# The start of a two-branch kernel: first input tile in halves on two queues, its transposes in four PSUM banks, identity built on chip, initial memory transposed behind the first tile, one norm put off

## Chip, cores and metric

One core of one Trainium2 chip. The metric is the device time of the whole program in microseconds (us); lower is better. Time before the change: median 1509.06 us of three runs when the prediction was made. All runs told here were classed as fast. The mean granted TensorE clock (the share of its full speed that the profile shows PE was allowed) was 1.0 in most; it was 0.994 to 0.999 in all runs of r3, r5 and r8, in three of five of r7, and in single runs of r4, r6 and of before. The profiled runs among these show what that mean hides: before the last microseconds, one stretch at half clock, of 3.4 us (10.2 us in r5), that begins during a wait of PE or within 1.2 us after one (waits of 0.9 to 9.5 us). Work that falls into 3.4 us at half clock is done 1.7 us later. Where this bears on a comparison it is said.

## The reference, cut to what matters

```python
def reference(A_x, A_mem0, A_Wq, ..., B_w1, B_w2, B_w3, B_w4):
    x = A_x                                   # (1, 2048, 1024) bf16
    xn = _layernorm(x)
    return x + _A_ref(xn, A_mem0, ...) + _B_ref(xn, B_w1, ...)

def _B_ref(x, w1, w2, w3, w4):                # gets xn, and norms it once more
    h  = _gelu(_layernorm(x) @ w1)            # 1024 -> 1024
    hs = shift_tokens(h) @ w2                 # four groups of columns, by -1, +1, -2, +2 tokens
    x1 = x + hs
    return x1 + _gelu(_layernorm(x1) @ w3) @ w4          # 1024 -> 3584 -> 1024

def _A_ref(x, mem0, Wq, Wk, Wv, Wo, seg_len): # attention by segments of 32 tokens,
    ...                                       # 8 memory rows handed from segment to segment, mem0 first
```

The kernel calls the first branch B and runs it first. I call its parts **stage one** (norm, transpose, times w1, GELU; 0 to 67 us), **stage two** (times w2, second norm; 67 to 122 us) and **stage three** (times w3 and w4, from 122 us on, with the first work of branch A in between). Branch A fills the rest up to 1504 us and is not touched, but for where its initial memory comes from. A tile is 128 tokens; there are 16.

## The kernel before

A tile of x goes through statistics on VectorE (DVE), one power -1/2 on GpSimd (POOL), and two norms: `norm2` (layer norm of the layer norm, the input of w1) and `norm1` (xn itself, kept in SBUF and also stored to a scratch in DRAM, for branch A). For tiles 0 to 5 TensorE (PE) transposes norm2's result against an identity; from tile 6 on a DMA does it, issued by SyncE (SP).

```python
    ident = const_tile("c_ident", np.eye(P, dtype=np.float32))     # loaded from DRAM
    load_consts(1)
    ...
    sums = cpool.tile([P, NTILE * 8, 4], F32)
    nc.gpsimd.memset(sums[:], 1.0)
    ...
    load_x(0)                                                      # SP's queue, one 128x1024 tile
    for c, q in ((0, nc.scalar), (2, nc.scalar), (1, nc.sync), (3, nc.sync)):
        if q is nc.sync:
            load_x(1 + c // 2)
        q.dma_start(w1_sb[:, 2*c:2*c+2, :], w1_v[:, 2*c:2*c+2, :])  # w1 in four quarters
    ...
    def norm_stats(n, part=None):
        ...
        nc.vector.scalar_tensor_tensor(ab[:], epsm[:], mv[:, 1:2], epsa[:], op0=ALU.mult, op1=ALU.add)
        nc.gpsimd.tensor_tensor(rr[:], ab[:], neghalf[:], op=ALU.pow)   # both columns at once

    def norm2(n, xn2T, jj):
        ...                                          # DVE for tiles 0-7, ScalarE (ACT) from tile 8 on
        if n >= NPE:                                 # NPE = 6
            nc.sync.dma_start_transpose(xn2T[:, jj], xn2[:])

    def norm1(n):
        ...
        nc.vector.tensor_scalar(xn, xts[n][:], mv[:, 0:1], rr[:, 0:1], op0=ALU.subtract, op1=ALU.mult)
        nc.gpsimd.dma_start(xn_v[:, n, :], xn)       # the store, 256 KB
        ...

    def transposes(xn2, xn2T, jj, half, halves=False):
        ps = psum0.tile([P, 4, P], F32, tag="tr")    # one bank for four transposes, two such banks
        for k in range(4):
            nc.tensor.matmul(ps[:, k, :], xn2[:, ...], ident[:], start=True, stop=True)
        step = 2 if halves else 4
        for i in range(0, 4, step):
            nc.scalar.copy(xn2T[:, jj, half*4+i:half*4+i+step, :], ps[:, i:i + step])
    ...
    def ahead(n):                                    # n = 6, 7
        norm_stats(n + 1, 0)
        norm2_of(n)
        norm_stats(n + 1, 1)
        norm1(n - 2)
    def prep(n):                                     # n = 8 .. 15
        norm2_of(n)
        norm_stats(n + 1)
        norm1(n - 2)
    ...
    def mem_start():                                 # in stage three, at about 219 us
        ps9 = psum3.tile([P, KT, M + 1], F32, tag="vr")
        for k in range(KT):
            nc.tensor.matmul(ps9[:, k, :], m0[:, k*P:(k+1)*P], eye9[:], start=True, stop=True)
        ...
```

## Time and profile before

| | before |
|---|---|
| time, median of 3 | 1509.06 us (1509.02 to 1513.19) |
| time, median of all 6 runs beside the changed kernel's | 1509.69 us |
| span of the profiled run | 1507.1 us |
| PE busy | 1497.1 us, 99% |
| waits of PE | three, all before 33 us |
| first weight matmul | 7.99 us |
| second tile's first weight matmul | 12.01 us |
| third wait of PE | 0.54 us, ends at 32.20 |
| stage two starts | 67.13 us |
| stage three starts | 122.39 us |

PE is the bound nearly everywhere, so a microsecond of this kernel is won only if PE starts its matmuls earlier, waits less between them, or has fewer of them. The lines of the profile are in the prediction and are not shown again. In a timeline line the columns are: start and busy time in us, engine, line of the kernel, operation, output<-input, shapes, count, and in brackets the idle time before it and what ended that. In a line of waits they are: engine, tile and line that waited, what it waited for, then us in total, number of waits and the longest.

### The profile page before, as it was taken

The page shows a single profiled execution, that of the slowest core. Times are in us where ns is not written, and L with a number is a line of the kernel's source. Part 1 is how long each engine was busy: PE and PEld are TensorE (multiplying, and loading weights), DVE is VectorE, ACT ScalarE, POOL GpSimd, SP SyncE. Part 2 cuts the span into 40 slices and gives each one's busy share as a digit, 9 for nine tenths or more (in the row PEclk, how much of TensorE's full clock was granted, in tenths as well). Part 3 has the DMA queues.
Part 4 walks back from the last instruction along what each step waited for, and adds up shares of the span by engine and source line. Part 5 has one row for each costly group of instructions (what it writes and reads, how often), then busy time and mean ns, then how long its engine had stood idle before and what let it go on. Part 6 is the DMA issues. An engine that isn't in the chain of part 4 may idle for free.

```text
span 1507.1 us, 24242 instructions
## 1 busy us (share of the span) xinstructions
PE 1497.1 (99%) x9757; PEld 803.3 (53%) x9828; DVE 546.9 (36%) x1146; ACT 502.0 (33%) x1140; POOL 176.6 (12%) x247
## 2 busy tenths in 40 slices
PE   9999999999999999999999999999999999999999
PEld 7844444445454444444456645664665455545555
DVE  8382230100010112211246624651564166516642
ACT  5533103013012011111156614650663166406630
POOL 5241020211211221100000000001000100010001
PEclk9999999999999999999999999999999999999999
DMA  9699752453445777622389956992997298918911
GB/s 307 156 272 321 218 174 89 137 203 111 155 155 144 188 236 252 218 98 84 126 219 262 238 128 174 255 239 72 240 251 203 72 230 217 223 63 207 209 49 51
DMA packets 305410, 272.93 MB, mean 181 GB/s; under 512 B 156054, under 2 KB 272312, under 8 KB 305296
## 3 DMA queue, kind: packets, MB, share of 16 engines
q1 hardware_dynamic: 282800, 189.38, 50.4%
q0 software_dynamic: 21808, 80.85, 15.4%
q8 instruction: 79, 1.29, 0.4%
q10 hardware_dynamic: 688, 1.11, 0.2%
q14 instruction: 35, 0.29, 0.1%
HBM read 190.08 MB, written 45.29 MB: 156 GB/s over the span
## 4 chain that ended last, share of the span: by engine, by line
PE 98%; DVE 1%; issue 0%; DMA 0%; ACT 0%; POOL 0%
PE ps L658 30%; PE ps L592 15%; PE pso L716 15%; PE ps L533 13%; PE ps L559 13%; PE ps L397 4%; PE ps L315 3%; PE psS L673 2%; PE psO L697 2%; PE ps L856 1%; PE ps L485 1%; PE gps L468 0%; PE ps L454 0%; DVE st L256 0%; DVE st L259 0%
## 5 line engine op out<-in xcount | busy, mean ns | idle before, releaser
L658 PE MATMUL ps<-hTb,wt 128*128 128x396 bf16 (+2 forms) x2528 | 484.9, 342 | 0.0
L658 PEld LDWEIGHTS <-wt 128*128 128x128 bf16 x2528 | 236.7, 98 | 175.7 <-DMA wt<-in_A_Wq_dram 0.4
L592 PE MATMUL ps<-wt,xT 128*128 128x512 bf16 x1004 | 220.1, 379 | 1.1
L716 PE MATMUL pso<-wo_sb,oX 128*128 128x512 bf16 (+1 forms) x972 | 208.3, 372 | 1.1
L533 PE MATMUL ps<-xn3T,w_sb 128*128 128x512 bf16 x896 | 196.2, 379 | 0.0
L559 PE MATMUL ps<-w_sb,h3T 128*128 128x512 bf16 x873 | 194.1, 379 | 1.2
L592 PEld LDWEIGHTS <-xT 128*128 128x128 bf16 x1024 | 100.2, 98 | 120.8
L534 ACT ACTIVATE h3T<-ps 128x512 bf16<-128x512 f32 x112 | 66.9, 597 | 291.1 <-PE ps L533 290.2
L716 PEld LDWEIGHTS <-oX 128*128 128x128 bf16 x992 | 96.3, 98 | 107.6
L660 ACT CAST KT<-ps 128x462 bf16<-128x462 f32 (+2 forms) x160 | 81.8, 511 | 202.8 <-PE ps L658 198.7
L559 PEld LDWEIGHTS <-h3T 128*128 128x128 bf16 x896 | 87.1, 98 | 103.6
L533 PEld LDWEIGHTS <-w_sb 128*128 128x128 bf16 x896 | 86.6, 98 | 102.0
L679 DVE TENSOR_REDUCE sums<-sm 99x4 f32<-99x396 f32 (+2 forms) x176 | 97.6, 555 | 114.9 <-ACT sm L677 114.9
L662 ACT ACTIVATE QT<-ps 128x462 bf16<-128x462 f32 (+2 forms) x160 | 83.9, 525 | 120.3 <-PE ps L658 106.2
L594 ACT CAST Vs<-ps 128x512 bf16<-128x512 f32 x64 | 37.5, 586 | 232.1 <-PE ps L592 223.5
L675 DVE TENSOR_TENSOR sm<-psS,c_mask_reg_sb 99x396 f32<-99x396 f32 x152 | 86.7, 571 | 72.0 <-PE psS L673 71.7
L598 DVE CAST Vs<-ps 128x512 bf16<-128x512 f32 x64 | 44.3, 692 | 171.6 <-PE ps L592 166.0
L677 ACT ACTIVATE sm<-sm 99x396 f32<-99x396 f32 (+2 forms) x176 | 92.8, 527 | 34.9 <-DVE sm L675 27.9
L685 DVE TENSOR_TENSOR Pn<-sm,rs 99x396 bf16<-99x396 f32 (+2 forms) x176 | 98.9, 562 | 6.4 <-DVE rs L681 0.5
L723 POOL DMA_DIRECT2D out_dram<-ot x30 | 16.4, 548 | 698.2 <-DVE ot L722 698.1
L560 DVE TENSOR_TENSOR R<-ps,R 128x512 f32<-128x512 f32 x32 | 22.0, 690 | 182.1 <-PE ps L559 172.5
L722 DVE TENSOR_TENSOR ot<-pso,Rt 128x512 bf16<-128x512 f32 (+1 forms) x33 | 22.2, 675 | 166.6 <-PE pso L716 162.3
(127 smaller groups left out, 1049.5 us busy)
## 6 DMA issues: line engine op xcount, KB each, us to landing
wt<-in_A_Wq_dram SPq DMA_DIRECT2D x76, 512.0 KB
wt<-in_A_Wk_dram SPq DMA_DIRECT2D x76, 512.0 KB
wt<-in_A_Wv_dram POOLq DMA_DIRECT2D x24, 1024.0 KB, 6.4
V_scratch<-Vs SPq DMA_DIRECT2D x32, 512.0 KB
V<-V_scratch SPq DMA_DIRECT2D x40, 384.0 KB
R_scratch<-x POOLq DMA_DIRECT2D x16, 512.0 KB, 4.1
R<-R_scratch SPq DMA_DIRECT2D x16, 512.0 KB
R_scratch<-R POOLq DMA_DIRECT2D x16, 512.0 KB, 3.5
```

Source lines behind the costliest of these rows:

```text
L533: nc.tensor.matmul(ps[:].rearrange("p (n t) -> p n t", t=P), w3_sb[:, k, f * P:(f + 1) * P], xn3T[tb][:, :, k, :], start=(k == 0), stop=(k ...
L534: nc.scalar.activation(h3T[:, f, :], ps[:], ACTF.Gelu_apprx_tanh)
L559: nc.tensor.matmul(ps[:], h3T[:, f, j * P:(j + 1) * P], w4_sb[:, f, ch * 512:(ch + 1) * 512], start=(f == 0), stop=(f == FT - 1))
L592: nc.tensor.matmul(ps[:], xT[:, m4 * 4 + j, k, :], wv[:, k, :], start=(k == 0), stop=(k == KT - 1))
L658: nc.tensor.matmul(ps[:, :nb], w[:, k, hh * P:(hh + 1) * P], B["hT"][:, k, :nb], start=(k == 0), stop=(k == KT - 1))
L660: nc.scalar.copy(dst[:, hh, :], ps[:, :nb])
L662: nc.scalar.mul(dst[:, hh, :], ps[:, :nb], scale)
L675: nc.vector.tensor_tensor(sm[:T, :, :T], S3, t["mask"][:].unsqueeze(1).to_broadcast((T, 4, T)), op=ALU.add)
L677: nc.scalar.activation(e[:T, :, :T], sm[:T, :, :T], ACTF.Exp, scale=LN2)
L679: nc.vector.tensor_reduce(ss, e[:T, :, :T], axis=AX.X, op=ALU.add)
L685: nc.vector.tensor_tensor(Pn[:T, :, :T], e[:T, :, :T], rs[:T, :].unsqueeze(2).to_broadcast((T, 4, T)), op=ALU.mult)
L716: nc.tensor.matmul(self.ps[:, :self.w], self.oX[0][:, h, self.oX[1] + self.gl * P:self.oX[1] + (self.gl + 1) * P], wo_sb[:, h, self.cc], s ...
```

## The change

The intent is to get PE to its first real matmul sooner, and to take eight small matmuls out of stage three. The diff, without the declarations:

```diff
-    ident = const_tile("c_ident", np.eye(P, dtype=np.float32))
-    load_consts(1)
-    eye9 = const_tile("c_eye9", ...)
+    ident = cpool.tile([P, P], BF16)
+    nc.vector.memset(ident[:], 1.0)
+    eye9 = cpool.tile([M, M + 1], BF16)
+    c0 = cpool.tile([P, KT, 1], F32)
...
-    nc.gpsimd.memset(sums[:], 1.0)
...
-                psum0 = ... tc.tile_pool(name="psum0", bufs=2, space=PSUM)
+                psum0 = ... tc.tile_pool(name="psum0", bufs=4, space=PSUM)
...
-                            nc.sync.dma_start(xts[n][:], x_v[:, n, :])
+                            if n == 0:
+                                nc.scalar.dma_start(xts[n][:, 512:], x_v[:, n, 512:])
+                                nc.sync.dma_start(xts[n][:, :512], x_v[:, n, :512])
+                            else:
+                                (nc.gpsimd if n == 12 else nc.sync).dma_start(xts[n][:], x_v[:, n, :])
+                    m0 = hTB[:M, 0, 16:16 + D]
+                    nc.gpsimd.dma_start(m0, A_mem0[0])
+                    nc.gpsimd.affine_select(ident[:], ident[:], [[-1, P]], ALU.is_equal, 0.0, base=0, channel_multiplier=1)
+                    nc.gpsimd.memset(eye9[:, M:M + 1], 1.0)
+                    nc.gpsimd.tensor_copy(eye9[:, 0:M], ident[:M, :M])
...
-                        nc.gpsimd.tensor_tensor(rr[:], ab[:], neghalf[:], op=ALU.pow)
+                        for c in (slice(1, 2), slice(0, 1)) if n == 0 else (slice(0, 2),):
+                            nc.gpsimd.tensor_tensor(rr[:, c], ab[:, c], neghalf[:, c], op=ALU.pow)
...                                                   # transposes():
-                        ps = psum0.tile([P, 4, P], F32, tag="tr")
-                        for k in range(4):
-                            nc.tensor.matmul(ps[:, k, :], ...)
                         step = 2 if halves else 4
                         for i in range(0, 4, step):
-                            nc.scalar.copy(..., ps[:, i:i + step])
+                            ps = psum0.tile([P, 4, P], F32, tag="tr")
+                            for k in range(step):
+                                nc.tensor.matmul(ps[:, k, :], ...)
+                            nc.scalar.copy(..., ps[:, :step])
...                                                   # behind tile 0's transposes:
+                    for k in range(KT):
+                        nc.tensor.matmul(ps9[:, k, :], m0[:, k * P:(k + 1) * P], eye9[:], start=True, stop=True)
                     norm_stats(1)
+                    nc.vector.tensor_copy(MZ[:, :, 0:M], ps9[:, :, 0:M])
+                    nc.vector.tensor_copy(c0[:], ps9[:, :, M:M + 1])
-                    load_consts(5)
+                    load_consts(4)
+                    nc.gpsimd.memset(sums[:], 1.0)
...                                                   # ahead(n):
-                        norm1(n - 2)
+                        if n == 6:
+                            norm1(n - 2)
...                                                   # prep(n):
+                        if n == 8:
+                            norm1(n - 3)
                         norm1(n - 2)
...                                                   # stage three:
+                    if n == 0:
+                        nc.vector.tensor_tensor(xb[:, :, 0:1], c0[:], xb[:, :, 0:1], op=ALU.add)
-                m0 = ...                              # and its load
-                def mem_start(): ...                  # and its call
```

`norm1(5)` is the norm put off: it now stands directly before `norm1(6)`.

> **What bounds the kernel now.** First the page of the profile: busy shares and the shares of the chain.
>
> ```profile
> PE 1497.1 (99%) x9757; PEld 803.3 (53%) x9828; DVE 546.9 (36%) x1146; ACT 502.0 (33%) x1140; POOL 176.6 (12%) x247
> PE 98%; DVE 1%; issue 0%; DMA 0%; ACT 0%; POOL 0%
> ```
>
> PE is busy for 1497.1 us of a span of 1507.1 us, so all that any rearrangement can win is about 10 us, or 0.7%. The change leaves the matrix work of the stages alone. Next I asked which waits of PE there are at all in the whole span:
>
> ```profile
> PE warm L332 <- DVE wz L326: 1.4, 1, 1.4
> PE ps L292 <- DVE xn L271: 0.8, 1, 0.8
> PE ps L315 <- ACT hTB L317: 0.5, 1, 0.5
> ```
>
> Three, and all lie in the first 33 us. The other idle time is a few ns between matmuls and the last 3 us (the output's way out), which the change does not touch. So the question is how early PE gets its real work, and what becomes of the third wait. The timeline of the head:
>
> ```profile
> 4.03 0.69 DVE L256 BATCH_NORM_STATS2 st<-xt 128x6 f32<-128x512 bf16 x1 [2.71 <-DMA xt<-in_A_x_dram]
> 5.91 0.73 POOL L262 TENSOR_TENSOR rr<-ab,neghalf 128x2 f32<-128x2 f32 x1 [3.30 <-DVE ab L261]
> 6.67 0.73 DVE L271 TENSOR_SCALAR xn<-xt,mv,rr 128x512 bf16<-128x512 bf16 x2 [0.85 <-POOL rr L262]
> 7.14 0.72 PE L292 MATMUL ps<-c_ident_sb,xn 128*128 128x128 bf16 x8 [0.79 <-DVE xn L271]
> 7.57 1.20 ACT L295 CAST xn2T<-ps 128x256 bf16<-128x256 f32 x4 [4.31 <-PE ps L292]
> 7.99 2.84 PE L305 MATMUL ps<-xn2T,w_sb 128*128 128x128 bf16 x48
> ...
> 12.20 0.53 POOL L130 DMA_DIRECT2D c_mask_sb<-c_mask  x1
> 12.74 0.74 POOL L262 TENSOR_TENSOR rr<-ab,neghalf 128x2 f32<-128x2 f32 x1
> ...
> 13.51 0.55 DVE L271 TENSOR_SCALAR xn<-xt,mv,rr 128x1024 bf16<-128x1024 bf16 x1 [0.75 <-POOL rr L262]
> ...
> 24.96 3.97 SPq L275 DMA_TRANSPOSE xn2T<-xn  x2
> ...
> 30.64 1.24 ACT L273 ACTIVATE xn<-xt,nm,rr 128x1024 bf16<-128x1024 bf16 x1 [2.05 <-DVE mv L260]
> ...
> 32.20 35.09 PE L315 MATMUL ps<-xn2T,w_sb 128*128 128x256 bf16 x320 [0.54 <-ACT hTB L317]
> ```
>
> The serial head is: x tile 0 lands at 4.01, two statistics, one power on POOL, the norm, transposes, a copy, and the first weight matmul at 7.99. After 13.51 DVE has no gap until 31 us. It feeds tiles 6 and 7, whose DMA transposes start at 24.96 and 27.64. By the semaphores in the trace these land at 30.54 and 31.88. ACT's norm of tile 8 starts 0.1 us after the first landing. The profile names DVE's aggregate as its releaser, but that ended at 30.61, after ACT's wait had already been answered by the landing. That norm (1.24 us) holds up the copies out of PSUM behind it on ACT, and PE resumes at 32.20, just after a copy that ended at 32.15. So the third wait hangs on DVE's chain through the DMA transposes. From 32.20 on PE runs without a gap: an earlier head is worth only as much as 32.20 moves.
>
> **What the Trainium skill says.** "DMA: Bandwidth & Descriptors", section "Issuing engines are not separate DMA queues": queues of several engines run on the same 16 DMA engines, and issuing from two saves only the sequencer's time. The trace agrees in part. The issues of x tile 0 (SP) and the first weights (ACT) both start at 0.76, yet between 2 and 3 us the transfers by queue are
>
> ```profile
> q1 hardware_dynamic: 85, 0.17, 75.0%
> q10 hardware_dynamic: 2, 0.00, 2.9%
> ```
>
> (q1 is SP's). ACT's queue moves only when SP's tile is nearly through.
>
> "GPSIMD Engine Reference", section "2.1 Instruction dispatch": each POOL instruction pays two software dispatches, and the first call to freshly loaded code about 6 us. The first half agrees: a power of two columns takes 0.70 to 0.98 us here, one of one column 0.56 to 0.57 (the third norm at 72 us and later). The second is not seen: POOL changes its configuration at 2.53, and the power still starts 0.08 us after its input at 5.82.
>
> "PSUM — Partial Sum Buffer", section "Terms": TensorE and ScalarE must not touch one bank at once. The trace agrees as far as it goes: the first copy starts at 7.57, after the fourth transpose of its bank ended at 7.53.
>
> "TensorE: Matmul & The Clock Gate", Part 1: full rate comes after some 3.4 us of activity. The 12 warming matmuls start every 0.43 us (slow), and the transposes at 7.14 take 219 ns (fast).
>
> **The change part by part.**
>
> *x tile 0 in halves.* It removes no bytes. The 128 rows took from 1.75 to 3.3 us on the wire, only some 85 a microsecond, against about 200 a microsecond later. Half rows might make the first half land some 0.3 us earlier, but there are twice as many rows, and the second half comes from the queue that started last. First statistic up to 0.3 us earlier; the second may wait for its half. I take 0.2 us won (estimate; -0.3 to +0.5 is open).
>
> *Power by column, the needed one first.* About 0.73 - 0.57 = 0.16 us won. The other column runs on POOL before tile 1's statistics are there (7.3 to 9.1 us), so it costs nothing.
>
> *Identity built on chip.* The loaded one landed at 6.62, 0.5 us before its use. It would have become a floor under any larger gain; by itself it wins nothing. The fill of 128x128 goes ahead of the warming fill on DVE (256 words took 0.27 us), so the warm-up ends some 0.1 us later, at about 6.6: still before the transposes at about 6.8.
>
> *Four banks.* The first copy can start after two transposes instead of four: 2 x 56 ns = 0.11 us earlier, 7.99 becomes 7.88.
>
> *Initial memory behind the first tile.* Eight tiny matmuls. Their cost in the old place, from the chain:
>
> ```profile
> 219.24 0.28 PE ps L442 x8
> ```
>
> With the issue step of 0.05 us about 0.33 us leave PE's gapless stretch: a true win. In the new place they stand on PE between the last transpose (its next slot is 7.69) and the first weight matmul: 7.69 + 0.28 = 7.97. They eat what the four banks won (7.97 against 7.99). DVE's two copies (0.21 and about 0.18 us) fit in its 0.82 us wait for tile 1's power.
>
> *POOL's order.* One small constant load (0.63 us) goes, the fill of the sums (0.71 us, formerly in the dead time at 1.90) comes in before tile 2's power, which already waits for POOL: 13.51 would come some 0.15 us later relative to the rest (2.27 + 0.71 against 2.81, with the first load of a row dearer). That is lost from DVE's chain.
>
> *Norm put off.* Tile 5's second norm (0.54 us) stands after tile 7's norm on DVE, so it does not move the two transposes. The chain shown by the profile runs through it, but I read ACT's wait as the landing. I give it 0.
>
> *x tile 12 by POOL's queue*: 0.6 us of POOL in a slack place; 0.
>
> Sum: DVE's chain 0.20 + 0.16 - 0.15 = 0.21 us earlier, and so 32.20 too; the extra 0.17 us by which PE's own head is ahead turns into a longer third wait (0.54 to 0.71). Plus 0.33 at 219 us: 0.54 us. To that I add some 0.3 us for the chance that the put-off norm or a luckier transpose shortens the third wait (at most 0.54 + 0.17). 1509.06 - 0.85 = 1508.2.
>
> **The rivals.**
>
> 1. *The third wait goes away.* For: the profile's chain names DVE, and the norm put off is 0.54 us of it. Against: the landing at 30.54 answers ACT's wait to 0.02 us. It would make 1507.5 to 1507.8.
> 2. *Halves land later than the whole.* For: ACT's queue starts about 1 us after SP's, and 256 half rows have to be described. Against: later rows pass at twice the rate. It costs up to 0.3 us: about 1508.8.
> 3. *POOL reloads code for the new select*, and the first power is late. For: the 6 us of the skill. Against: not seen here, and POOL has some 2.5 us of slack between about 3.0 and 5.5. If it happens: 1510 to 1512.
> 4. *Weights become the floor.* The last pair of w1 lands at 10.83, used at 11.12: only 0.3 us of slack at the first tile's sixth step. It cuts PE's own lead, which is lost in the third wait anyway: nothing.
>
> **Range and chances.** The parts span about -0.5 to +2 us, which is 1507 to 1509.5. The three runs of before show one at 1513.19 beside 1509.02 and 1509.06, so the upper side gets a little more: 1506.8 to 1509.8. Two per cent are 30 us: three times all the idle time of PE, so faster is as good as excluded; slower would need PE kept from work for 30 us, which no moved wait can do. Faster 0.003, within 2% 0.99, slower 0.007.
>
> **What would show it.** Right: PE still has three waits; the first weight matmul at about 7.5 to 7.7; tile 2's norm at 13.2 to 13.4; the third wait near 0.7 us with PE's gapless run starting at about 32.0; nothing of the eight matmuls at 219 us. Wrong: a second statistic that waits for the DMA, a power more than 0.1 us after its input, a third wait that is gone, or a wait of PE later than 33 us, which would mean that the rearranged loads or the put-off norm hit a stage I hold untouched.

## The result, and the profile after

| | before | after |
|---|---|---|
| time, median of 6 runs each | 1509.69 us (1509.02 to 1513.19) | 1509.15 us (1508.83 to 1510.23) |
| profiled run | 1509.15 us | 1509.85 us |
| first statistic on DVE | 4.03 us | 3.46 us |
| first weight matmul | 7.99 us | 7.35 us |
| second tile's first weight matmul | 12.01 us | 12.01 us |
| PE's wait at 32 us | 0.54 us | none |
| PE's wait at 39 us | none | 1.49 us |
| stage two starts | 67.13 us | 68.08 us |
| stage three starts | 122.39 us | 123.34 us |
| start of stage three to the first matmul behind the memory's old place | 109.17 us | 108.78 us |
| last matmul starts | 1503.44 us | 1504.04 us |

The ratio of the fast runs is 0.9994, with a 95% interval of 0.9981 to 1.0007: the time is the same. (Ratios and intervals are those of the measuring program, from the fast runs; they are not quite the ratios of the medians.) The profiled run of after is one of its slower ones, 0.7 us above its median, and that of before is 0.54 us below the median of before. So the table's last lines, in which after is 0.60 us *later*, are not the medians' difference; they show how large one wait was in one run.

The kernel after, busy time and shares of the chain that ended last:

```profile
PE 1496.9 (99%) x9757; PEld 803.2 (53%) x9828; DVE 546.9 (36%) x1148; ACT 502.2 (33%) x1140; POOL 175.5 (12%) x250
PE 97%; DMA 1%; DVE 1%; issue 0%; POOL 0%; SPq 0%; POOLq 0%
```

The kernel after, waits of PE over the whole span:

```profile
PE ps L326 <- DMA xn2T<-xn: 1.5, 1, 1.5
PE warm L343 <- DVE wz L337: 1.5, 1, 1.5
PE ps L305 <- DVE xn L281: 0.4, 1, 0.4
PE ps L316 <- DMA w_sb<-in_B_w_dram: 0.2, 1, 0.2
```

PE's work is what it was (1496.9 against 1497.1 us). Of its three waits the one for the first norm has shrunk from 0.8 to 0.4 us, the third, for ACT, is gone. In its place stands a wait of 1.5 us for a DMA transpose (`xn2T<-xn`), and a small one for w1. The 0.4 us does not measure the gain, since the warm-up matmuls before it ended at another time.

The kernel after, timeline of the head:

```profile
3.46 0.69 DVE L265 BATCH_NORM_STATS2 st<-xt 128x6 f32<-128x512 bf16 x1 [2.04 <-DMA xt<-in_A_x_dram]
...
5.94 0.73 DVE L281 TENSOR_SCALAR xn<-xt,mv,rr 128x512 bf16<-128x512 bf16 x2 [0.69 <-POOL rr L272]
...
6.41 0.72 PE L305 MATMUL ps<-ident,xn 128*128 128x128 bf16 x8 [0.39 <-DVE xn L281]
...
7.06 0.35 PE L360 MATMUL ps<-eye,hTB 8*128 8x9 bf16 x8
...
7.35 1.07 PE L316 MATMUL ps<-xn2T,w_sb 128*128 128x128 bf16 x16
...
8.64 1.96 PE L316 MATMUL ps<-xn2T,w_sb 128*128 128x128 bf16 x32 [0.23 <-DMA w_sb<-in_B_w_dram]
...
11.10 1.07 PE L316 MATMUL ps<-xn2T,w_sb 128*128 128x128 bf16 x16
...
12.01 2.40 PE L326 MATMUL ps<-xn2T,w_sb 128*128 128x128 bf16 x40
...
12.87 0.55 DVE L281 TENSOR_SCALAR xn<-xt,mv,rr 128x1024 bf16<-128x1024 bf16 x1 [0.42 <-POOL rr L272]
```

Read it from the top. Everything up to the first weight matmul is 0.57 to 0.73 us earlier than before: first statistic 4.03 to 3.46, norm 6.67 to 5.94, weight matmul 7.99 to 7.35. But PE then waits for w1's quarters, at 8.64 and again at 11.10 (its weight loads waited 0.23 us for the same tile there), and the second tile starts at 12.01, to the hundredth where it was. PE's own lead is used up after 4 us. DVE's lead is not: tile 2's norm starts at 12.87 instead of 13.51, 0.64 us earlier, and so the first DMA transposes are issued at 24.30 and 26.97 instead of 24.96 and 27.64. In this run tiles 6 and 7 then landed at 29.68 and 31.02 (before: 30.54 and 31.88), and PE has no wait at 32 us (before: 0.54 us). (Landing times are the last semaphore update of a DMA in the packed trace; `prof` doesn't print them for transposes.)

Then comes the new wait. The kernel before, stores of tiles 5 and 6, and the kernel after, timeline from 28 us on:

```profile
30.32 0.61 POOL L282 DMA_DIRECT2D xn_scratch<-xnk  x1 [0.20 <-issue]
...
32.47 0.62 POOL L282 DMA_DIRECT2D xn_scratch<-xnk  x1 [0.20 <-issue]
```

```profile
31.32 1.16 POOL L292 DMA_DIRECT2D xn_scratch<-xnk  x2 [0.21 <-issue]
...
40.14 12.06 PE L326 MATMUL ps<-xn2T,w_sb 128*128 128x256 bf16 x109 [1.49 <-DMA xn2T<-xn]
```

PE needs tile 9's transpose. It was issued at 32.99, 0.86 us earlier than before (33.85), and landed at 40.01, 1.14 us later (38.87): 7.0 us instead of 5.0. The line of POOL at 31.32 shows what lies beside it: two stores of normed tiles issued back to back (tile 5's at 31.32 and tile 6's at 31.93; before they were issued at 30.32 and 32.47). By their landing times up to four stores were in flight at once beside tile 9's transpose, where before it was up to three.

In stage three the eight matmuls are gone from the chain (before, they stood between the 22 and the 56):

```profile
215.28 4.91 PE ps L572 x22
220.19 12.09 PE ps L546 x56
```

The bookkeeping of these two profiles closes: waits 1.49 - 0.54 = +0.95 us, which is also the delay of stage two (68.08 - 67.13); then 109.17 - 108.78 = 0.39 us won; +0.56 in sum, against +0.60 at the last matmul.

### The profile page after: what moved, and what is told of

Read it like the earlier page. It is cut to its first block, busy times and chain, and to the rows that moved or that the text cites. A ratio compares the mean times of both kernels' runs of the same rounds, so it can differ in the third digit from the quotient of the medians.

```text
span 1507.5 us, 24248 instructions
## 1 busy us (share of the span) xinstructions
PE 1496.9 (99%) x9757; PEld 803.2 (53%) x9828; DVE 546.9 (36%) x1148; ACT 502.2 (33%) x1140; POOL 175.5 (12%) x250
## 4 chain that ended last, share of the span: by engine, by line
PE 97%; DMA 1%; DVE 1%; issue 0%; POOL 0%; SPq 0%; POOLq 0%
PE ps L669 30%; PE ps L603 15%; PE pso L727 15%; PE ps L546 13%; PE ps L572 13%; PE ps L417 4%; PE ps L326 2%; PE psS L684 2%; PE psO L708 2%; DMA w_sb<-in_B_w_dram 1%; PE ps L867 1%; PE ps L498 1%; PE gps L481 0%; PE ps L467 0%; DMA xn2T<-xn 0%
```

## The experiments

**The theory** after this reading (S): the head's gain reaches DVE's chain and takes the old third wait away, but the DMA transposes of tiles 8 to 10 run beside the stores of the normed tiles, which stretch them; the stall at 39 us is that, and the put-off norm, which puts two stores side by side, makes it worse. **Rivals**: the transposes, of which up to three are under way at once, slow each other (T); the halves of x tile 0 push the queue back and with it w1 and the later tiles (H); the order of x's loads decides (O); the stretch is chance, and another run of the same kernel shows none (C). All kernels gave correct results. Four went to a chip together, with shared runs of before: the first two sets of four on one chip, the third on another. So r9 to r12 were never run beside the changed kernel; they are compared with each other and with before.

### The same kernel once more (r1_same)

No edit.

> The changed kernel once more, to see how far its one profile is typical. Theory S (the put-off norm lets two stores of normed tiles start back to back, 0.6 us apart, and these delay the DMA transposes of tiles 8 and 9): PE waits for tile 9's transpose again, 1.2 to 1.8 us at about 38.6 us, and the landing is again near 40.0. Theory L (luck of the DMA engines): the wait is anything from 0 to 1.8 us. Both: first weight matmul at 7.3 to 7.5, the first stage's second tile at 12.0, time 1508.8 to 1509.9.

Measured: 1509.01 us (median of 5, 1508.69 to 1510.04) against 1509.63 of before in the same set; ratio 0.9995 (0.9982 to 1.0008). From the waits of PE in this run:

```profile
PE ps L326 <- DMA xn2T<-xn: 1.1, 1, 1.1
```

Tile 9's transpose took 33.28 to 39.73, 6.4 us, and PE resumed at 39.87. The wait is there again, 0.4 us smaller: not mere chance (against C), though its size varies.

### The norm put back (r2_norm_back)

```diff
-                        if n == 6:
-                            norm1(n - 2)
+                        norm1(n - 2)
...
-                        if n == 8:
-                            norm1(n - 3)
```

> The changed kernel with tile 5's second norm back in its old place, after tile 7's norm. Theory S: the two stores are 2 us apart again, tile 9's transpose lands by 39.0, PE's wait for it shrinks from 1.5 to under 0.5 us, and the time is 0.8 to 1.4 us below that of the changed kernel (about 1508.0). Theory L: no difference beyond 0.5 us, with a wait of any size. My prediction's step (the norm put off is worth nothing) says the same as L: within 0.3 us.

Measured: 1508.76 us (1508.19 to 1509.72), ratio 0.9993 (0.9980 to 1.0006). The stores are apart again (29.6 and 31.78), tile 9's transpose takes 5.2 us, the wait at 39 us is gone. But in this run tile 6's transpose took 6.5 us (5.4 in after), and PE waited 0.63 us at 32 us, although DVE was as early as in after (tile 2's norm at 12.86). Stage two starts at 67.42, against 67.81 in the repeat and 68.08 in after. The times, 1508.76 and 1509.01, overlap in their ranges. So the put-off norm does put two stores beside the transposes that stall, and the single profiles speak for a cost of 0.4 to 0.7 us; the time does not settle it.

### The stores of tiles 4 to 15 issued together after the last norm (r3_stores_late)

```diff
-                        nc.gpsimd.dma_start(xn_v[:, n, :], xn)
+                        if n < 4:
+                            nc.gpsimd.dma_start(xn_v[:, n, :], xn)
...                                        # behind the last norm1
+                    for n in range(4, NT):
+                        nc.gpsimd.dma_start(xn_v[:, n, :], xn_keep[n // 4][:, n % 4])
```

> The changed kernel with the stores of normed tiles 4 to 15 put off to the end of the first stage, so that no store runs beside the DMA transposes. Theory S: the transposes of tiles 8 and 9 take 4 to 5 us from issue to landing instead of 6.1 and 7.0, no wait of PE is left after 12 us, and the time is 1.3 to 1.6 us below the changed kernel (about 1507.6). Theory L, or a third cause (the transposes slow each other): landing times as before, a wait of 0.5 to 1.8 us, time within 0.5 us of the changed kernel.

Measured: 1516.06 us (1515.00 to 1517.65), ratio 1.0042 (1.0029 to 1.0055). Slower by 6.4 us, 0.4%, clear of the noise. The largest wait of PE in this kernel, which ends at 66 us:

```profile
PE ps L327 <- DMA xn2T<-xn: 5.7, 1, 5.7
```

The stores were issued from 44.6 us on, while transposes were still under way, because the last norms on DVE run ahead of the transposes. Where no store ran, tiles 8 to 10 took 3.0, 3.1 and 3.1 us, though they were issued as close together as in after (1.9 us apart), with two under way at once: against T. (Tile 11 took 4.7 us, also without a store; what held it is open.) Beside the stores, up to eight of them at once, tile 14 took 49.72 to 61.00 (11.3 us) and tile 15 took 53.40 to 65.93 (12.5 us). (Tile 15 has loads of w3 beside it in every kernel and takes 5.5 to 6.4 us in before and after; tile 14 takes 3.2 and 3.1.) So the dose goes with the effect, roughly: no store, mostly 3 us; two to four at once, 3.5 to 7.0 (tiles 8 to 11 of before and after); up to eight, 6.0 for tile 13 and 11 to 13 for tiles 14 and 15. Not all of the 6.4 us is this wait: the clock was at half from 65.4 to 68.8 us, and, as in r2, a wait of 0.58 us stood at 32 us, where tile 6 had taken 6.3 us. The plan failed as a speed-up, because I took the stores' place in the program for their place in time.

### Tile 0 loaded whole (r4_whole_tile)

```diff
-                            if n == 0:
-                                nc.scalar.dma_start(xts[n][:, 512:], x_v[:, n, 512:])
-                                nc.sync.dma_start(xts[n][:, :512], x_v[:, n, :512])
-                            else:
+                            if True:
                                 (nc.gpsimd if n == 12 else nc.sync).dma_start(xts[n][:], x_v[:, n, :])
```

> The changed kernel with x tile 0 again as one load of the SP queue. If the halves won what the profiles say: first statistic at 4.0 instead of 3.46, first weight matmul about 0.55 later, at 7.9, DVE's chain 0.5 later too. If the weights are the floor that swallowed it: PE's wait for the second and fourth pair of weights (0.45 us in all) goes, the second tile's weights still start at 12.0 to 12.1, and the time differs only by what the transposes' waits do, within 0.6 us of the changed kernel. If the head mattered for the end, the time would be 0.6 us longer.

Measured: 1509.51 us (six runs, 1508.56 to 1513.72), ratio 1.0002 (0.9990 to 1.0015). The head of this kernel:

```profile
4.00 0.69 DVE L262 BATCH_NORM_STATS2 st<-xt 128x6 f32<-128x512 bf16 x1 [2.58 <-DMA xt<-in_A_x_dram]
...
7.89 2.85 PE L313 MATMUL ps<-xn2T,w_sb 128*128 128x128 bf16 x48
```

The halves alone are worth 4.00 - 3.46 = 0.54 us at the first statistic and 7.89 - 7.35 = 0.54 us at the first weight matmul. And PE's lead is worth nothing: without the halves the first, second, third and fourth quarter of w1 to land do so 0.5 to 0.9 us earlier (5.12, 7.98, 8.54, 10.58 against 6.01, 8.60, 9.45, 11.06), the first tile has no wait for weights, and the second tile starts at 11.92, no later than with them (12.01). What the halves win is DVE's chain alone (tile 2's norm at 13.41, in after 12.87). This kernel still has a wait of 0.60 us for ACT at 32 us, which the profile of the changed kernel has not. And it has the new wait too, 0.73 us up to 40.05 us, for tile 9, whose transpose took 6.1 us. So the stall doesn't need the halves (against H).

The queues between 2 and 3 us show why the half lands sooner. Columns: packets, MB, share of the 16 engines' time. The kernel after:

```profile
q1 hardware_dynamic: 131, 0.13, 39.9%
q10 hardware_dynamic: 116, 0.11, 33.7%
```

The kernel with tile 0 whole:

```profile
q1 hardware_dynamic: 100, 0.20, 87.4%
q10 hardware_dynamic: 14, 0.03, 7.6%
```

As much is moved in all (0.24 and 0.23 MB). With halves, both queues carry tile 0; without, ACT's queue (q10) carries what little of w1 passes. So the tile is pulled ahead of w1, and w1 pays with the same half microsecond.

### Stores of tiles 4 to 15 spread over stage two (r5_stores_stage2)

The edit of r3, but the stores stand in stage two's loop, two to a tile:

```diff
                         nc.gpsimd.dma_start(R1_v[:, n, :], x1[:])
+                        for m in (2 * n + 4, 2 * n + 5):
+                            if m < NT:
+                                nc.gpsimd.dma_start(xn_v[:, m, :], xn_keep[m // 4][:, m % 4])
```

> The changed kernel with the stores of normed tiles 4 to 15 moved into the second stage, two behind each of its first six tiles, where no transpose of the first stage is in flight. Theory S (stores beside the DMA transposes stretch them): all transposes from tile 8 on land 3 to 4.5 us after their issue (as where no store ran in the run with late stores: 3.0 to 3.1), PE's wait near 38.5 us is gone, only the one at 31.5 (about 0.6) may stay, the second stage starts at about 67.2 instead of 67.8 to 68.1, and the time is 0.6 to 0.9 us below the changed kernel. Rival (the stores only move the trouble): a new wait of PE in the second or third stage, because the second stage has transposes of its own; time as before or above.

Measured: 1517.55 us (1514.96 to 1520.33), ratio 1.0051 (1.0038 to 1.0065). The gain in stage one is there: tiles 8 to 14 take 3.0 to 3.8 us each, PE has no wait at 32 or 39, stage two starts at 66.17 (68.08 in after) and stage three at 121.42. Then it is lost several times over:

```profile
PE ps L550 <- ACT h3T L551: 9.5, 1, 9.5
```

(PE then worked at half clock up to 141.8 us.) The line names ACT, but ACT stood behind the norm of a late tile: this chain of the same kernel shows that two stage-two transposes took 27 us together and a later one 13 us.

```profile
91.39 27.43 DMA xn3T<-xn x2
...
123.12 13.00 DMA xn3T<-xn
```

Stage two transposes every tile by DMA too, beside its own stores of x1; twelve more stores are too much there.

### Order of x's loads (r6_x2_last)

```diff
-                        if q is nc.sync:
-                            load_x(1 + c // 2)
+                        if c == 1:
+                            load_x(1)
...
-                    for n in range(3, 7):
+                    for n in range(2, 7):
```

> The changed kernel with x tile 2 loaded behind the last quarter of w1 instead of ahead of it. If the weights are the floor that swallowed the earlier head: the last quarter lands 0.6 us earlier, at about 10.4 instead of 11.06, and the second tile's weights start at 11.4 to 11.6 instead of 12.0. If something else holds tile 0's last sixteen matmuls (tile 1's transposes, done at 10.9), the start stays at 11.8 to 12.0. For the end: tile 2's statistics start 0.6 to 1.3 us later, so tiles 6 and 7 land later too and PE's wait at 31.5 comes back; I expect the time within 0.5 us of the changed kernel, so a lead at 12 us buys nothing.

Measured: 1509.85 us (1509.49 to 1512.47), ratio 1.0001. w1's last quarter landed at 10.12 instead of 11.06, tile 0's 64 weight matmuls took 4.16 us with no wait (4.66 in after), and the second tile started at 11.87 instead of 12.01. But x tile 2 came late, DVE's chain with it (tile 2's norm at 13.46, in after 12.87), and PE waited 0.33 us at 32 and

```profile
41.11 4.12 PE L326 MATMUL ps<-xn2T,w_sb 128*128 128x256 bf16 x21 [2.11 <-DMA xn2T<-xn]
```

In these kernels, what goes in front of w1 delays PE, and what goes behind it delays DVE. (This run's warm-up was also slow to reach the full clock, so its first weight matmul was at 7.71; part of the comparison is confounded by that.) Against O as a cure.

The profiled run is the slowest of the five, 2.5 us above the next, because this wait cost more than itself. The window behind it, with the granted clock as the third number from the end:

```profile
41.40:44.70 3.30, 3.30 (x17) 2.33 (x16) 3.23 (x9) 0.56 (x2) 2.50 (x5) 0.50 0.97 273
```

The clock was at half from 41.36 to 44.77, 1.7 us lost. Stage two starts at 70.72, 2.64 us later than in after: 0.95 us more of waits from 32 us on (0.33 + 2.11 against 1.49) and these 1.7. No run shows how long a wait must be for this: those of 1.49 us in after and of 1.09 in r1 were not followed by a half clock.

### The memory's move alone, in the kernel before (r7_mem_only)

The memory is loaded at the start on POOL's queue, behind the loaded identity and `eye9`, and its eight matmuls and two copies stand behind tile 0's transposes, as in the change; `mem_start` goes.

```diff
+                    m0 = hTB[:M, 0, 16:16 + D]
+                    nc.gpsimd.dma_start(m0, A_mem0[0])
...                                            # behind tile 0's transposes
+                    for k in range(KT):
+                        nc.tensor.matmul(ps9[:, k, :], m0[:, k * P:(k + 1) * P], eye9[:], start=True, stop=True)
+                    nc.vector.tensor_copy(MZ[:, :, 0:M], ps9[:, :, 0:M])
+                    nc.vector.tensor_copy(c0[:], ps9[:, :, M:M + 1])
...
-                def mem_start(): ...            # and its call
```

> The kernel before with nothing but the initial memory's transposition moved behind the first tile (its load too). My prediction's step: 0.29 us less between the start of the third stage and the first group that follows the old place, PE's first weight matmul of tile 0 0 to 0.3 us later, at most 12.3 for the second tile; the third wait as before (0.5 to 1.2 us). Time 0.3 us below before, give or take what the transposes do (0.5 us). Rival: the eight matmuls' time is not on the path (PE waits elsewhere in the third stage for as long): the stretch around the old place stays the same.

Measured: 1510.45 us (1508.18 to 1510.98), ratio 1.0002.

```profile
8.66 0.35 PE L352 MATMUL ps<-c_eye_sb,hTB 8*128 8x9 bf16 x8 [0.92 <-DMA hTB<-in_A_mem_dram]
```

Here the memory landed only at 8.61, as its load stood third in POOL's queue, and PE waited 0.92 us for it. In the change that load is first in the queue and lands at 6.19; whether the identity built on chip is needed for that, or only another order of the loads, was not tried. Then the clock was at half from 9.4 to 12.8 us, and the first 48 weight matmuls took 4.48 us (2.84 in before). The second tile starts at 14.60, not by 12.3 as expected, and the third wait is gone: PE came to it 2.6 us later, and tile 2's norm stands at 12.88 (before: 13.51), as one load less is in front of its power on POOL. Three of the five runs have a clock of 0.999 (1510.45 to 1510.98 us), the two with 1.0 took 1508.18 and 1509.11; so the median says little about the move. In stage three the step is 108.78 us, as in after: 0.39 us won, whatever else differs.

### The stores in stage two, in the kernel before (r8_before_stores2)

The edit of r5 on before.

> The kernel before with the stores of normed tiles 4 to 15 moved into the second stage, as in r5. Theory S: tiles 6 and 7 still land at about 30.5 and 31.9 or a little earlier, the wait near 32 stays at 0.2 to 0.6 us, nothing appears at 39, and the time is 0 to 0.5 us below before. Against r5 it tells what the change's head is worth once the stores are out of the way: r5 should be 0.3 us (the eight matmuls) to 0.8 us (plus a smaller third wait) below r8.

Measured: 1524.16 us (1516.58 to 1528.66), ratio 1.0100 (1.0084 to 1.0115). Stage one gains nothing here (stage two starts at 67.26, before 67.13), because the wait at 32 us hangs on DVE's late chain (0.79 us), and there was no wait at 39 us to remove. Between 122 and 138 us PE then loses 5.5 us in four waits (two for ACT, 2.8 us; one for w3, 2.4 us; one for DVE, 0.3 us) and works at half clock up to 139.5. This profiled run is the fastest of the five; the others took 7 to 12 us longer, at a mean clock of 0.994 to 0.996.

### Stores held back until the last transpose is used (r9_stores_gated)

From the failures of r3 and r5: the stores must run after stage one's last DMA transpose and before stage two's first one. A small copy on POOL reads one element of the GELU output of tile 14 (written by the last matmul group of stage one), which holds POOL's queue until then.

```diff
-                        nc.gpsimd.dma_start(xn_v[:, n, :], xn)
+                        if n < 4:
+                            nc.gpsimd.dma_start(xn_v[:, n, :], xn)
...                                        # behind the last norm1
+                    gate = big.tile([1, 1], BF16)
+                    nc.gpsimd.tensor_copy(gate[:], hTB[0:1, 0, 2 + (NT - 2) * P:3 + (NT - 2) * P])
+                    for n in range(4, NT):
+                        nc.gpsimd.dma_start(xn_v[:, n, :], xn_keep[n // 4][:, n % 4])
```

> The changed kernel with the stores of normed tiles 4 to 15 started when the first copy of stage one's last pair of tiles is done (about 60 us), that is after the last transpose of stage one has landed and before the first of stage two is issued at 74 us. Theory S: transposes of tiles 8 to 14 land 3.0 to 3.8 us after issue, PE has no wait over 0.3 us between 12 us and the end of stage one, stage two starts at 66.2 to 66.4 (changed kernel 67.8 to 68.1), nothing is lost later, and the time is 1.5 to 1.9 us below the changed kernel: 1507.2 to 1507.6. Rival: the stores run into stage two's transposes and weights again and give back part or all, as in r5.

Measured: 1508.17 us (1507.61 to 1508.56), against 1509.93 of before in the same set (ten runs, 1508.49 to 1517.01); ratio 0.9989 (0.9975 to 1.0002). All waits of PE over the whole span of this kernel:

```profile
PE warm L344 <- DVE wz L338: 1.5, 1, 1.5
```

One wait is left, that of the warm-up before any data is there. The run of matmuls that the waits at 32 and 39 us broke is whole, from 27.8 to 66.3 us. Tiles 7 to 14 take 3.0 to 3.7 us. Tile 6 takes 5.4 us and tile 15 takes 6.6, beside loads of x and of w3, and in r11, where no store at all runs beside them, 5.5 and 6.8: so it seems that loads stretch a transpose too, but here nothing is late for it. The expectation overrated the whole: 1.5 to 1.9 us below the changed kernel were expected, and the medians differ by 0.98 us (0.84 from r1), on another chip. The ranges don't overlap (r9 at most 1508.56, after and r1 at least 1508.69). The stores are issued from 61.1 to 67.0 us and have landed by 73.4; the first transpose of stage two is issued at 74.3. Stage two starts at 66.32. DMA queues between 30 and 50 us, the kernel after (q0 is POOL's, the stores):

```profile
q1 hardware_dynamic: 6468, 2.28, 66.3%
q0 software_dynamic: 875, 2.88, 44.1%
```

The gated kernel, the same stretch (there is no q0):

```profile
q1 hardware_dynamic: 6752, 2.33, 55.2%
```

SP's queue, which carries the transposes and a few loads, moves the same bytes, but its packets take less of the engines' time, and there is nothing beside it.

### The same stores held back, in the kernel before (r10_before_gated)

The edit of r9 on before.

> The kernel before with the stores started late in the same way. Theory S: stage two starts at 67.0 to 67.3, with the one wait of 0.5 to 0.8 us at 31.5 left (tiles 6 and 7 are not helped, as in r8), third stage at 122.4; time 1509.0, within 0.4 us of before. Then r9 against r10 is the worth of the changed kernel's head when the stores are out of the way: 0.4 (eight matmuls) + 0.5 to 1.0 (no wait at 31.5, the start of tile 1's weights) = 0.9 to 1.4 us. Rival (the head's worth is zero in any case): r9 and r10 differ by 0.4 us only.

Measured: 1509.33 us (1509.00 to 1510.05), ratio 0.9996 (0.9983 to 1.0010). Its transposes are short too (3.0 to 3.7 us for tiles 8 to 14), yet

```profile
PE ps L316 <- ACT hTB L318: 1.3, 1, 1.3
```

the wait at 32 us is still there, as it hangs on DVE's chain and on tile 6, which took 6.3 us and landed at 31.19 in this run (the wait is larger than the 0.5 to 0.8 us expected). So the change, with the stores out of the way on both sides, is worth 1509.33 - 1508.17 = 1.16 us, of which 0.39 is the memory's move, and the ranges do not overlap. That is the answer to where the change's gain went: it is real, and with the stores in place only about half of it shows (0.54 us between the medians of before and after, 0.62 in r1).

### All sixteen stores held back (r11_gated_all)

r9 with all stores behind the gate (`if n < 4` becomes never, the loop starts at 0).

> As r9, but all sixteen stores wait, so none runs beside tile 6's transpose or the last x loads either. Theory S: tile 6's transpose lands 4 to 4.5 us after issue instead of 5.1 to 5.7, tile 7's as in r9; PE had no wait there in r9, so the time is that of r9 within 0.4 us, unless four more stores (1 MB[...]) reach stage two's first transposes.

Measured: 1508.15 us (1507.79 to 1511.08), ratio 0.9988 (0.9974 to 1.0001). The median is that of r9: no harm of the first four stores shows. Tile 6's transpose took 5.5 us, not the 4 to 4.5 expected: it is not these stores that make it long. The profiled run is the slow one of the five; PE waited 3.0 us for w3 at 147 to 151 us in it. Stage two's transposes took 11.7 to 16.9 us from 102 to 126 us in it (3.3 to 6.4 in r9), long after the last store had landed (76.1); why stays open.

### The gate, with the norm put back (r12_gated_norm_back)

The edits of r9 and r2 together.

> As r9, with tile 5's second norm back in its old place. If the put-off norm acted only through its store (what r2 suggests), it is worth nothing here: no wait at 38.5, at 31.5 a wait of at most 0.2 us, stage two's start within 0.3 us of r9's, the time within 0.4 us. If it acted through DVE's chain (0.54 us less in front of tile 8's norm on ACT), the wait at 31.5 of about 0.6 us comes back, and the time is 0.5 us above r9.

Measured: 1508.20 us (1507.73 to 1509.06), ratio 0.9990 (0.9976 to 1.0004), against r9's 1508.17. There is no wait at 32 or 39 us in it. (Stage two starts at 66.77, 0.45 us later than in r9; 0.26 of it is there already when the second tile starts, after a wait of 0.41 us for w1.) With the stores out of the way no difference shows when the norm is done. So the put-off norm, if it acts at all, acts through the place of its store, not through DVE's time.

## Why the prediction was right or wrong, point by point

The time came out inside the range (1509.15, predicted 1508.2, 1506.8 to 1509.8), "the same" was right, and for the main reason given: PE is 99% busy and the change leaves its work alone. That reason alone makes "the same" nearly certain, so it tests none of the parts. The prediction's own signs decide those: the first weight matmul and tile 2's norm came earlier than the stretches given for "right" (7.35, 12.87), and two of the signs of being wrong came true, a third wait that is gone and a wait later than 33 us. Of the steps some held and one failed, and it is partly luck that the total fits: two errors hid each other.

**Halves: 0.2 us predicted, 0.57 measured** (4.03 to 3.46; 0.54 by r4). The term was mis-sized: I took a gain on the wire of 0.3 us and discounted it for a late second half. The second statistic does not wait for its half (it follows at 4.07, one statistic later). The rival "halves land later than the whole" is refuted.

**Power by column: 0.16 predicted, 0.16 measured**: DVE's wait before the norm went from 0.85 to 0.69 us.

**Four banks and memory: right.** The first copy starts 0.33 us after the first transpose instead of 0.43, so 0.10 us against 0.11; the eight small matmuls (7.06, 0.35 us) fill the place up to 7.35, so the banks' gain is eaten, as said, and 0.09 us more. From first transpose to first weight matmul it is 0.94 us now and was 0.85.

**DVE's chain: 0.21 us earlier predicted, 0.64 measured** at tile 2's norm. It is the sum of the terms above, and of POOL's order, which cost 0.08 us where I said 0.15: from tile 1's norm to tile 2's it is 3.68 us, before 3.60. That cost hides two larger parts. In r7, where one load leaves POOL's place in front of that power and no fill comes in, it is 3.08: so the load gone won 0.5 us and the fill of the sums took 0.6 back.

**PE's own lead: lost, but elsewhere.** I had it turn into a longer wait at 32 us. It was lost before, to w1's quarters at 8.64 and 11.10 us, as rival 4 has it ("weights become the floor", nothing lost). r4 shows the cause: tile 0 overtakes w1 in the queues. Rival 3 (POOL loads code for the new select, the 6 us that the prediction quotes) did not happen: the first power started 0.09 us after its input (5.34, 5.25).

**The third wait: the step that failed.** "The extra 0.17 us by which PE's own head is ahead turns into a longer third wait (0.54 to 0.71)" and "From 32.20 on PE runs without a gap". In fact DVE's chain gained 0.64 us and PE's nothing, and the wait of 0.54 us vanished; rival 1 happened. That took luck as well: in r2 and r3, with nearly the same lead of DVE (norms at 12.86 and 12.92), tile 6's transpose took 6.5 and 6.3 us instead of 5.4, and waits of 0.63 and 0.58 us were back. And the gain was not kept. A new wait of 1.49 us (1.09 in the repeat) came at 39 us. I read in the trace when the transposes of tiles 6 and 7 landed; I did not ask how much time those behind them had left, nor what shared the DMA engines with them. The landing of tile 9 at 38.87 in before was just early enough. r3, r5 and r9 show that the stores stretch the transposes, from mostly 3.0 to 3.8 us without them to as much as 7.0 (and 12.5 in r3).

**The norm put off: "I give it 0".** On DVE it is 0 (r12 against r9). With the stores in place its store moves next to tile 6's, and the profiles of r2 and r1 speak for a small cost; the times do not resolve it. The 0.3 us added "for the chance that the put-off norm or a luckier transpose shortens the third wait" had the wrong sign.

**Initial memory in stage three: 0.33 predicted, 0.39 measured**, in every profile without it in which PE has no other wait there (all but r5 and r11).

**Open**: whether the cost of the put-off norm is real; how far the transposes' length scatters from run to run (tile 6 landed between 28.9 and 31.2 us in the kernels here, wider than what was to be won); why single runs of before reach 1511 to 1517 us. For the two slowest with a clock on record (1513.51 and 1517.01) the mean clock is 0.998, where the others have 1.0. So they too probably had a stretch at half clock behind a wait, as r6's profile has; what PE waited for was not kept.

## What to carry to other kernels

An earlier start is worth what the next place where two chains meet lets through: here PE's lead ended at the weights 4 us on, and only DVE's lead counted. Ask of every transfer behind the wait that you remove how early it lands and what it shares the DMA engines with; here a store without any deadline delayed a transpose with one, and holding the stores back to a stretch without transposes brought out what the change is worth, 1.16 us (r9 against r10). Against the kernel before it is 1508.17 to 1509.93 us, a gain of 0.1% whose interval still touches nothing gained. Moving such stores by their place in the program failed twice here (1516 and 1518 us); making them wait for an event worked. And count a wait of PE at more than its length: one of 2.11 us cost 1.7 us more, because the clock was at half behind it (r6).

## What the Trainium skill lacked or had wrong

- "DMA: Bandwidth & Descriptors", section "Rules for kernel authors", says that a transpose next to ordinary DMAs needs nothing. That holds for the data (all results were correct), but it gives no price in time for that: a 256 KB transpose took 3.0 us from issue to landing with no ordinary DMA beside it (tiles 10 to 13 of r9), 3.4 to 7.0 us beside 256 KB stores of which at most two to five were in flight at once (tiles 8 to 13 of before, after and r1), and 11.3 us (tile 14 of r3, 3.0 in r9) beside up to eight. The queues' lines at r9 fit packets that take turns (352 bytes a packet on the mean on SP's queue, 2.28 MB in 6468, against 3.3 KB on the storing one, 2.88 MB in 875), but no run isolates that as the cause.
- The same page, section "Issuing engines are not separate DMA queues", says that issuing from several engines only saves the sequencer's time. At this program's start it saved more: a tile of 256 KB in halves on two queues landed at 3.44 and 3.64 us, whole on one queue at 3.98 (r4), because the second queue then carried the tile instead of weights (its packets were half as long, too; no run separates the two). The weights landed 0.5 to 0.9 us later for it, so the total rate did not rise (0.24 and 0.23 MB between 2 and 3 us): that part of the page agrees.
- No page has the durations of the small POOL operations that set this head: a power of one column of 128 rows took 0.55 to 0.57 us, of two columns 0.70 to 0.98, and the select that makes the 128x128 identity 0.32.
